# The leading expert's rows gathered after 15 of 20 chunks, the others' tokens placed from SBUF by one-hot matmuls

## Chip, cores and metric

The kernel runs on one core of a Trainium2 chip. The metric is the device time of one execution, in microseconds; the median of three runs is given. A profiled execution of its own gives the trace, and that execution's time stands beside the span of its trace.

## What is computed

Retention attention, then a mixture of experts with one expert per token and a limit of tokens for each, then a gated MLP. Shapes: 4 batches, 8 heads, 576 positions, 64 wide; 2304 tokens of 512; 8 experts with 1024 hidden columns; an MLP with 2048.

```python
def _attn_ref(q, k, v):
    scores = np.matmul(q, k.transpose(0, 1, 3, 2)) / np.sqrt(D_)
    Dmat = np.where(rel >= 0, gamma[:, None, None] ** rel[None], 0.0)
    return np.matmul(scores * Dmat[None], v)

def _moe_ref(x, w_gate, w1, w2, capacity):        # capacity = 2304 // 8 * 2
    logits = x @ w_gate
    expert_idx = np.argmax(logits, axis=1)
    ...                                           # gate_w: softmax at expert_idx
    for i in range(N):
        e = expert_idx[i]
        if counts[e] < capacity:
            disp[e, counts[e]] = x[i]
            pos[i] = counts[e]; counts[e] += 1; keep[i] = True
    h = np.maximum(np.einsum('ecd,edf->ecf', disp, w1), 0.0)
    y = np.einsum('ecf,efd->ecd', h, w2)
    out[i] = gate_w[i] * y[expert_idx[i], pos[i]] # for each kept token

def _moe2_ref(x, w_in, w_out):
    h = x @ w_in
    return (h / (1.0 + np.exp(-1.702 * h))) @ w_out
```

## The kernel before

**Attention.** The tokens go through in 20 chunks `n` (four batches of 128, 128, 128, 128 and 64). SP loads each chunk's q and k (`qk`) and its k and v (`kv`) into buffers that go round, six of each (`load`, L262); POOL scales them (`emit_Q`, L324 and L325). On PE, iteration `n` runs SC of chunk n+1 (scores), XO and KV of chunk n (output and state; the part that comes from the state, L368, is St), and XR of chunk n-1, which transposes the chunk into rows and multiplies it by the gate matrix `iw` in one go (L378). From XR's result DVE takes maxima (`mn`, `lg`), ACT the exponentials (`emit_EX`), and ACT scales the row by its gate weight and writes it to DRAM, tensor `xd` (`emit_ST`). XR of the last chunk takes the PSUM banks that held scores.

**Routing.** Chunks are routed in groups of 5, 5, 5, 3 and 2 (`GROUPS`). `gate1` makes the one-hots of the experts (`OH`). `gate2` counts the tokens ahead of each one by matmuls with a triangle and with ones (`pr`), adds the counts of the groups before (`base`), and makes two factors `A` and `Bt` of one-hots. In `gate3` a few matmuls `ix` multiply these, which puts each token's number at its expert's slot, and DVE adds it to `acc`. With the last group come the index tiles: `IDX0` for the leading expert, `IDX1` for the others, sorted by size (`sort_experts`). The leading expert is fixed by the counts of the first three groups (`lead`, LEAD = 2), so that SP can load its weights; the others come in order of their counts. `pad` strews these steps between the others of the loop; it takes no time of PE but that of the few matmuls.

**Experts.** An expert has a fixed width (`WR`: 370 columns for the first, 344 for the second, ...). POOL gathers its rows out of `xd` with three indirect DMAs (`gather`, L654). PE transposes them into columns (L780 for the first expert, L662 for the others), ACT and DVE split these into a rounded part `xh` and a remainder `xl` (`xevac`). There are 8 steps `fc` for each expert. A step `s` runs `L1` of step s+1 (12 matmuls, L682) and then `L2` of step s (12 matmuls, L701), with weights split in the same way: `split1`, `split2`: ACT casts, `a`, and DVE subtracts, `b`. L1's result is split by ACT (`hi`) and DVE (`lo`). `L2` adds its products up in four banks over the 8 steps (`acc`), and `yevac` takes them out. `load_w(e + 1, fc)` has ACT issue the loads of the next expert's weights, one of eight blocks in each step. Ahead of the first step ACT and DVE load the experts' offsets into registers (`offr`, L786), seven each.

**`compact`.** During the first expert, tokens are also given their places in the sorted order (`PERM`), step by step by `fill(place, 1)` ahead of each L1 and `fill(place, 2)` behind each L2: some 15 operations on DVE, then for each chunk a one-hot of 128 columns (L755, on DVE) and a matmul with it (L758), in a spare corner of `acc`'s first bank:

```python
            for g in range(0, NT + 2, 2):
                for n, (tag, bufs) in zip(range(g, min(g + 2, NT)), (("cu", 3), ("cab", 2))):
                    ...
                    nc.vector.tensor_scalar(As[n], iota, r3[:, n:n + 1], None, op0=ALU.is_equal)
                for n in range(max(g - 2, 0), g):
                    C = CH[n % NC]
                    nc.tensor.matmul(pp, As[n][:C], b2[:C, n, :], start=False, stop=n == NT - 1, skip_group_check=True)
                yield
```

Then the MLP runs over three blocks of 768 tokens, and its rows go out by indirect DMA. Every engine works its instructions off in the order of the program; nothing orders them anew at run time.

Of the kernel before, what the change touches and what calls it, by code (L numbers as in the profile page):

```python
# [1 line left out]

# [29 lines left out]
ZROW = N  # L32
# [5 lines left out]
NW = 3  # L38
# [15 lines left out]
def _consts():  # L54

    if _CONST:
# [10 lines left out]
    valid = np.array([[p < CH[c] for c in range(NC)] for p in range(P)])  # L67
# [9 lines left out]
             ("ca", ca), ("cb", cb), ("ids", ids), ("idz", ids - ZROW), ("idp", np.stack([ids // 16, ids % 16], 2)),  # L77
             ("izp", np.stack([(ids - ZROW) // 16, (ids - ZROW) % 16], 2)), ("iota", iota), ("thr", P * (iota[:, :NR] + 1)),
# [14 lines left out]
def fused(ctx: ExitStack, tc, qk, kv, wg, w1, w2, cap, w_in, w_out, cf, out):  # L93
# [32 lines left out]
    o_s, n_s = at["ca"][0], sum(at[x][1] for x in ("ca", "cb", "ids", "idz", "idp", "izp", "iota", "thr", "e7", "lt8", "tw"))  # L126
# [9 lines left out]
    idz, iota, thr, e7 = table("idz"), table("iota"), table("thr"), table("e7")  # L136
# [93 lines left out]

    with ExitStack() as a:
# [19 lines left out]
        one = acst.tile([P, P], BF16, name="one")  # L251
        St = [acst.tile([P, NP, P], F32, name=f"St{i}") for i in range(3)]
# [7 lines left out]
        def load(n):  # L260
# [23 lines left out]
        nc.gpsimd.memset(acc, float(ZROW))  # L284
# [16 lines left out]
        at_t, xT_t, mn_t, kv_t, xr_t = {}, {}, {}, {}, {}  # L301
# [25 lines left out]
        def emit_SC(n):  # L327
# [4 lines left out]
            sc = ps.tile([P, 2, NP, P], F32, tag="sc", name="sc")  # L332
# [9 lines left out]
        def emit_KV(n):  # L342
# [3 lines left out]
            if c == 0:  # L346
                kv_t[0] = ps.tile([P, NP, D], F32, tag="kv", name="kv")
# [725 lines left out]
```

## Time and profile before

| | |
|---|---|
| median of three runs | 770.02 us (769.84 to 770.62) |
| the profiled execution | 769.79 us, its span 768.0 us |
| TensorE clock granted, mean | 0.983 of full |
| PE busy | 735.1 us, 96% of the span |
| DVE, ACT, POOL busy | 504.4, 353.6, 104.9 us |

The trace holds one execution. Times in it count from the span's start. A stretch's granted clock is a mean share of full speed; 0.50 is the lower of TensorE's two levels, 1.2 of 2.4 GHz. A busy time holds an instruction's latency too, so that two in a row overlap, and the spacing of their starts is shorter.

### The profile page before, as it was taken

The numbers are of one execution on the slowest core, as the hardware profiler recorded it, in microseconds if no ns is written. First come the engines' busy times: TensorE is split into PE (matmuls) and PEld (weight loads), VectorE is DVE, ScalarE is ACT, GpSimd is POOL, SyncE is SP. The second block draws the span as 40 slices with busy tenths as digits, with TensorE's granted clock in tenths as the row PEclk, the third lists the DMA queues.
The fourth block names the chain that finished last, engine by engine and source line by source line (L and its number), as shares of the span: only waits on it lengthen the run. The fifth ranks groups of instructions, "written<-read, shape, count | busy, mean of one in ns | idle before, by whom it ended". The sixth has DMA issues, their size and how long they took to land.

```text
span 768.0 us, 13390 instructions
## 1 busy us (share of the span) xinstructions
PE 735.1 (96%) x4912; PEld 675.2 (88%) x4912; DVE 504.4 (66%) x1233; ACT 353.6 (46%) x754; POOL 104.9 (14%) x120
## 2 busy tenths in 40 slices
PE   6999939999999999999999999999999999999995
PEld 5898828999999999999999999999999988888884
DVE  4455667688988989998988888444434444433442
ACT  4554424365565665665444444433333344333332
POOL 3985025011010010000000000030000012000003
PEclk9999958999999999999999999999999999999998
DMA  9986554366777877867122120020000001000002
GB/s 325 333 294 239 197 166 140 96 216 204 246 220 201 263 241 226 264 219 240 60 68 67 57 70 29 0 83 1 1 0 1 1 18 65 1 1 1 1 0 86
DMA packets 42966, 94.90 MB, mean 124 GB/s; under 512 B 5783, under 2 KB 11031, under 8 KB 42896
## 3 DMA queue, kind: packets, MB, share of 16 engines
q1 hardware_dynamic: 22432, 45.39, 18.1%
q10 hardware_dynamic: 16752, 38.72, 15.8%
q0 software_dynamic: 3712, 9.88, 3.6%
q8 instruction: 41, 0.67, 0.4%
q14 instruction: 29, 0.24, 0.1%
HBM read 79.81 MB, written 14.16 MB: 122 GB/s over the span
## 4 chain that ended last, share of the span: by engine, by line
PE 44%; issue 33%; DVE 5%; POOL 3%; DMA 1%; ACT 1%; ACTq 0%; another core or an unknown queue 0%; DVEq 0%; POOLq 0%
PE h L682 12%; PE acc L701 12%; PE h L854 9%; PE y L879 8%; POOL out L892 2%; PE tx L662 1%; DVE b L633 1%; DMA xg<-xd,IDX 1%; DVE lo L687 1%; DVE b L642 1%; DMA cs<-in_moe_w_in 0%; POOL xg L654 0%; ACT a L632 0%; DVE cab L219 0%; DVE ct L730 0%
## 5 line engine op out<-in xcount | busy, mean ns | idle before, releaser
L860 DVE TENSOR_TENSOR sg<-h,sg 128x384 f32<-128x384 f32 (+1 forms) x96 | 53.4, 557 | 130.7 <-ACT sg L859 130.7
L859 ACT ACTIVATE sg<-h 128x384 f32<-128x384 f32 (+1 forms) x96 | 47.2, 491 | 164.6 <-PE h L854 164.5
L879 PE MATMUL y<-b,gh 128*128 128x512 f32 x288 | 112.5, 391 | 0.0
L879 PE MATMUL y<-a,gl 128*128 128x512 f32 x288 | 112.4, 390 | 0.0
L879 PE MATMUL y<-a,gh 128*128 128x512 f32 x288 | 112.2, 390 | 0.0
L854 PE MATMUL h<-yh,a 128*128 128x384 f32 (+2 forms) x384 | 82.7, 337 | 0.0
L854 PE MATMUL h<-yh,b 128*128 128x384 f32 (+2 forms) x384 | 82.7, 337 | 0.0
L854 PE MATMUL h<-yl,a 128*128 128x384 f32 (+2 forms) x384 | 82.6, 337 | 0.0
L862 ACT CAST gh<-sg 128x384 fp32r<-128x384 f32 (+1 forms) x96 | 49.3, 513 | 71.6 <-DVE sg L860 71.6
L633 DVE TENSOR_TENSOR b<-w1r,a 128x512 fp32r<-128x512 f32 x112 | 77.0, 687 | 7.6 <-ACT a L632 6.4
L701 PE MATMUL acc<-hi,a 128*128 128x370 f32 (+7 forms) x256 | 80.2, 313 | 0.0
L863 DVE TENSOR_TENSOR gl<-sg,gh 128x384 fp32r<-128x384 f32 (+1 forms) x96 | 53.6, 558 | 39.0 <-ACT gh L862 31.2
L701 PE MATMUL acc<-lo,a 128*128 128x370 f32 (+7 forms) x256 | 79.0, 308 | 0.1
L701 PE MATMUL acc<-hi,b 128*128 128x370 f32 (+7 forms) x256 | 78.8, 308 | 0.0
L641 ACT CAST a<-w2r 128x512 fp32r<-128x512 f32 x112 | 69.0, 616 | 20.4 <-PE acc L701 19.3
L642 DVE TENSOR_TENSOR b<-w2r,a 128x512 fp32r<-128x512 f32 x112 | 76.7, 685 | 1.0 <-ACT a L641 1.0
L892 POOL DMA_INDIRECT out<-ob,PERM x18 | 17.8, 990 | 435.2 <-ACT ob L889 431.9
L854 PEld LDWEIGHTS h<-yh,a 128*128 128x128 f32 x384 | 68.2, 188 | 9.1 <-ACT yh L706 0.2
L632 ACT CAST a<-w1r 128x512 fp32r<-128x512 f32 x112 | 69.3, 619 | 12.5 <-issue 3.0
L854 PEld LDWEIGHTS h<-yh,b 128*128 128x128 f32 x384 | 66.4, 188 | 2.7
L854 PEld LDWEIGHTS h<-yl,a 128*128 128x128 f32 x384 | 66.1, 188 | 2.8
L879 PEld LDWEIGHTS y<-a,gl 128*128 128x128 f32 x288 | 54.1, 188 | 11.4
(160 smaller groups left out, 1263.7 us busy)
## 6 DMA issues: line engine op xcount, KB each, us to landing
w1r<-in_moe_w ACTq DMA_DIRECT2D x28, 512.0 KB, 4.4
w2r<-in_moe_w ACTq DMA_DIRECT2D x28, 512.0 KB, 4.0
qk<-in_qk SPq DMA_DIRECT2D x16, 512.0 KB, 6.4
kv<-in_kv SPq DMA_DIRECT2D x16, 512.0 KB, 6.9
cs<-in_moe_w_in SPq DMA_DIRECT2D x32, 256.0 KB, 3.2
cs<-in_moe_w_out SPq DMA_DIRECT2D x32, 256.0 KB, 3.0
xd<-xrow ACTq DMA_DIRECT2D x16, 256.0 KB, 5.4
w1r<-in_moe_w SPq DMA_DIRECT2D x4, 512.0 KB, 5.6
```

What stands on the lines that cost most here:

```text
L632: nc.scalar.copy(a, s)
L633: nc.vector.tensor_tensor(b, s, a, op=ALU.subtract)
L641: nc.scalar.copy(a, s)
L642: nc.vector.tensor_tensor(b, s, a, op=ALU.subtract)
L682: nc.tensor.matmul(h[:, :n], wt[:, kc, :], xs[e, kc][j][:, :n], start=i == 0, stop=i == 3 * KC - 1)
L701: nc.tensor.matmul(y[dc][:, :n], wt[:, dc * P:(dc + 1) * P], x[:, :n], start=fc == 0 and i == 0, stop=fc == NF - 1 and i == 2)
L854: nc.tensor.matmul(h[:, :n], wt[:, kc, :], x[:, kc, o:o + n], start=i == 0, stop=i == 3 * KC - 1)
L859: nc.scalar.activation(sg[:, :n], h[:, :n], AF.Sigmoid, scale=1.702)
L860: nc.vector.tensor_tensor(sg[:, :n], h[:, :n], sg[:, :n], op=ALU.mult)
L862: nc.scalar.copy(gh[:, :n], sg[:, :n])
L863: nc.vector.tensor_tensor(gl[:, :n], sg[:, :n], gh[:, :n], op=ALU.subtract)
L879: nc.tensor.matmul(accs[bi][c // P + t], x[:, t * P:(t + 1) * P], wt, start=f == 0 and i == 0, stop=f == 2 * NF - 1 and i == 2)
```

## The change

The groups are now 5, 5, 5 and 5 chunks. For the first three nothing changes but that their `gate3` comes an iteration earlier. `gate3` of the third group, in iteration 17 behind XR(16), now makes IDX0 and has POOL gather the leading expert's rows from these 15 chunks' part of `xd`. The zero row, which empty slots read, moves to the front of `xd`, so that it lies in that part.

The last five chunks' rows of the leading expert don't pass through DRAM. Their scaled rows `xrow` stay in SBUF (five buffers instead of three), DVE makes the one-hots `A0` of the slots (from 216 on, 154 slots), and PE adds `xrow` transposed times `A0` into the same banks into which it transposes the gathered rows. The remaining routing of the last group (`late_route`: 29 DVE operations, five `ix` matmuls, IDX1 and the sort) runs within the first expert, ahead of `compact`.

```diff
-GROUPS = [(0, 5), (5, 5), (10, 5), (15, 3), (18, 2)]
+GROUPS = [(0, 5), (5, 5), (10, 5), (15, 5)]
+NLEAD = sum(CH[n % NC] for n in range(sum(GROUPS[LEAD])))
+SLEAD = NLEAD // E
...
-            t = rows.tile([P, 2 * DM], F32, tag="qk", name="qk", bufs=6)[:, :2 * NP * C]
+            t = rows.tile([P, 2 * DM], F32, tag="qk", name="qk", bufs=5)[:, :2 * NP * C]
...
-            t = rows.tile([P, 2, H, D], F32, tag="kv", name="kv", bufs=6)
+            t = rows.tile([P, 2, H, D], F32, tag="kv", name="kv", bufs=4)
...
             v.tensor_tensor(acc, acc, ix[:, 1], op=ALU.add)
...
+            if g == LEAD:
+                n = [P, NW, E]
+                ts = sm.tile(n, F32, tag="ts", name="ts", bufs=1)
+                slot = sm.tile([P, NW], F32, tag="slot", name="slot", bufs=1)
+                v.tensor_tensor(ts, top[:, None, :].to_broadcast(n), acc.rearrange("p (e t) -> p t e", t=NW), op=ALU.mult)
+                v.tensor_reduce(slot, ts, op=ALU.add, axis=AX.X)
+                v.tensor_copy(IDX[0], slot)
+                gather(0, xd[:1 + NLEAD, :])
+        def rows_of_lead(x, kc):
+            for t in range(NW):
+                m = min(P, W - t * P)
+                if (t + 1) * P <= SLEAD:
+                    nc.tensor.transpose(x[:, t * P:t * P + m], xg[0, t][:m, kc * P:kc * P + P], ident[:m, :m])
+                else:
+                    nc.tensor.matmul(x[:, t * P:t * P + m], xg[0, t][:m, kc * P:kc * P + P], ident[:m, :m], start=False, stop=False, skip_group_check=True)
...
         emit_EX(NT - 2)
-        emit_ST(NT - 2)
         emit_XR(NT - 1)
-        g = len(GROUPS) - 1
+        emit_EX(NT - 1)
         gate1(g)
-        emit_EX(NT - 1)
-        emit_ST(NT - 1)
...
-        work.append(gate2(g))
-        pad(99)
-        gate3(g)
+        oht = sm.tile([P, KM, E], F32, tag="t", name="oht")[:, :k]
+        v.tensor_tensor(oht, OH[:, t0:t0 + k], top[:, None, :].to_broadcast([P, k, E]), op=ALU.mult)
+        for n in (NT - 2, NT - 1):
+            emit_EY(n)
+        for n in (NT - 2, NT - 1):
+            emit_ST(n)
+        tx0 = [psa.tile([P, 512], F32, tag=f"acc{i}", name="tx0") for i in range(2)]
+        for kc in range(2):
+            rows_of_lead(tx0[kc], kc)
+        pr = ranks(g)
+        rk = RK[:, t0:t0 + k]
+        v.tensor_tensor(rk, pr[:, :k, :], base[:, None, :].to_broadcast([P, k, E]), op=ALU.add)
+        v.tensor_tensor(oht, oht, rk, op=ALU.mult)
+        sl = sm.tile([P, KM], F32, tag="sl", name="sl")[:, :k]
+        v.tensor_reduce(sl, oht, op=ALU.add, axis=AX.X)
+        v.scalar_tensor_tensor(sl, sl, capf, sl, op0=ALU.is_lt, op1=ALU.mult)
...
+        for i, m in ((0, 2), (2, k - 2)):
+            v.tensor_tensor(A0[:, i:i + m], late_s[:, None, :].to_broadcast([P, m, SL]), sl[:, i:i + m, None].to_broadcast([P, m, SL]), op=ALU.is_equal)
...
+        for kc in range(2, KC):
+            rows_of_lead(tx0[kc], kc)
+        for kc in range(KC):
+            for i in range(k):
+                C = CH[(t0 + i) % NC]
+                nc.tensor.matmul(tx0[kc][:, SLEAD:W], xrow_t[t0 + i][:C, kc * P:kc * P + P], A0[:C, i], start=False, stop=i == k - 1, skip_group_check=True)
...
+            for n0, m in ((0, 8), (8, 8), (16, 4)):
...
+                nc.vector.tensor_tensor(A, iota[:, None, :].to_broadcast([P, m, P]), wide(r3, P)[:, n0:n0 + m], op=ALU.is_equal)
...
-        gather(0)
-        place = compact()
+        place = chain(late_route(), compact())
...
-            load_w(e + 1, fc)
+            for i in (fc,) if e else {3: (0, 1), 4: (2, 3), 5: (4, 5), 6: (6,), 7: (7,)}.get(fc, ()):
+                load_w(e + 1, i)
...
             if s < NF:
-                fill(place, 1)
+                fill(place, 5 if s < 3 else 2)
...
             if s < NF:
-                fill(place, 2)
+                fill(place, 5 if s < 3 else 2)
+            if s == 2:
+                gather(1, xd[:, :])
```

What the diff leaves out: `ranks` is the part of `gate2` with the `pr` matmuls; the exponentials of `emit_EX` and the two operations behind them are now `emit_EX` and `emit_EY`; `slots_late` fills the slot numbers `late_s` once, at n = 4. Attention and experts share PSUM banks now: scores, the XR of chunk 18, and two of the four results of an expert take turns in one tile of two banks (`acc2`), `kv` and `xo` in the banks of the other two results. The very first L1 takes its matmuls kc by kc. The registers `offr` are loaded in step 7. The path for tokens above an expert's width changes only in the number of the zero row.

On PE, at the end of attention, what stood between the last XR (L378) and the first L1 (L682) was the index matmuls (L529) of the fourth group, the ranks (`pr`) and index matmuls of the fifth, and the 12 transposes:

```order
L378 MATMUL xr<-iw,xT 64x136 x4
L529 LDWEIGHTS A
L529 MATMUL ix<-Bt,A 128x48
...
L468 MATMUL pr<-OH,tri 128x16
...
L529 MATMUL ix<-Bt,A 128x48
L780 MATMUL tx_1557<-ident,xg 128x128
...
L780 MATMUL tx_1560<-ident,xg 128x114
L682 MATMUL h<-xh,a_1545 128x370 x4
```

Now the transposed rows of kc 0 and 1 stand behind the last XR (L414), ahead of the ranks; those of kc 2 and 3 (`tx_1487`, two banks) and the placement matmuls (L654) stand behind them, ahead of the first L1 (L704):

```order
L414 MATMUL xr<-iw,xT 64x136 x4
L561 MATMUL tx_1459<-ident,xg 128x128
L563 MATMUL tx_1459<-ident,xg 128x128
L563 MATMUL tx_1459<-ident,xg 128x114
...
L482 MATMUL pr<-OH,tri 128x40
...
L561 MATMUL tx_1487<-ident,xg 128x128
...
L654 MATMUL tx_1459<-A_1483,xrow 128x154 x5
L654 MATMUL tx_1460<-A_1483,xrow 128x154 x5
L654 MATMUL tx_1487<-A_1483,xrow 128x154 x10
L704 MATMUL h<-xh,a_1532 128x370
```

So no index matmul stands between attention and the first expert any longer, and the gathered rows do so ahead of the ranks.

On DVE, in the first expert, the end of step 4 and step 5 were, with the weight remainders (L633, L642), `lo` (L687) and the one-hots of four and of two chunks (L755):

```order
L633 TENSOR_TENSOR b_1750<-w1r,a_1749 128x512
L642 TENSOR_TENSOR b_1754<-w2r,a_1753 128x512
L748 TENSOR_TENSOR ct<-ct,sml 128x720
L687 SCALAR_TENSOR_TENSOR lo<-h,hi 128x370
L755 TENSOR_SCALAR A<-sml,r 128x128 x4
L633 TENSOR_TENSOR b_1799<-w1r,a_1798 128x512
L642 TENSOR_TENSOR b_1803<-w2r,a_1802 128x512
L755 TENSOR_SCALAR A<-sml,r 128x128 x2
L687 SCALAR_TENSOR_TENSOR lo<-h,hi 128x370
L755 TENSOR_SCALAR A<-sml,r 128x128 x4
```

Now, at the same two steps, the last operations of `compact` ahead of the one-hots (L825, L828) come only there, and the one-hots (L844) in batches of eight chunks:

```order
L245 TENSOR_TENSOR b_1799<-w1r,a_1798 128x512
L671 TENSOR_TENSOR b_1803<-w2r,a_1802 128x512
L825 TENSOR_TENSOR ct<-r,sml 128x360
L828 TENSOR_TENSOR ct<-ct,sml 128x720
L709 SCALAR_TENSOR_TENSOR lo<-h,hi 128x370
L844 TENSOR_TENSOR A<-sml,r 128x1024
L245 TENSOR_TENSOR b_1843<-w1r,a_1842 128x512
L671 TENSOR_TENSOR b_1847<-w2r,a_1846 128x512
L844 TENSOR_TENSOR A<-sml,r 128x1024
```

So DVE comes to the first one-hot a step and more later, and then does eight chunks at once.

On POOL, ahead of the second expert's gather (indices `IDX_71`), the memset of `yl` stands now where a part of that gather stood, and the first gather (`IDX_70`) is issued behind the last scaling of kv (L361):

```order
L325 TENSOR_TENSOR kv<-kv,tab 128x512
L324 TENSOR_TENSOR qk<-qk,gqs 128x256
L325 TENSOR_TENSOR kv<-kv,tab 64x512
L386 MEMSET mn 128x1
L654 DMA xg<-xd,IDX_70 128x512 x2
L654 DMA xg<-xd,IDX_70 114x512
L654 DMA xg<-xd,IDX_71 128x512 x2
L654 DMA xg<-xd,IDX_71 88x512
L784 MEMSET yl 128x10592
```

```order
L422 MEMSET mn 128x1
L360 TENSOR_TENSOR qk<-qk,gqs 128x256
L361 TENSOR_TENSOR kv<-kv,tab 64x512
L260 DMA xg<-xd,IDX_70 128x512 x2
L260 DMA xg<-xd,IDX_70 114x512
L870 MEMSET yl 128x10592
L260 DMA xg<-xd,IDX_71 128x512 x2
```

So the memset no longer waits behind gathers of the second expert.

## Rows read from the trace of the kernel before

**Rows 1.** Windows: PE, PEld, DVE, ACT, POOL busy, clock, DMA share, GB/s.
```profile
0.00:98.00 98.00, 88.54 (x1227) 81.18 (x1227) 54.28 (x202) 47.98 (x128) 51.43 (x59) 0.99 0.81 280
98.00:116.60 18.60, 6.09 (x31) 4.21 (x29) 11.08 (x57) 4.42 (x12) 5.12 (x5) 0.59 0.46 145
116.60:120.20 3.60, 3.54 (x11) 3.34 (x12) 1.88 (x4) 1.07 (x3) 3.32 (x2) 0.50 0.23 77
160.00:768.00 608.00, 599.04 (x3414) 550.24 (x3412) 407.35 (x897) 282.51 (x579) 34.92 (x51) 0.99 0.31 97
```

**Rows 2.** Timeline of PE: start, us, instruction, what ended the idle time before.
```profile
88.50 1.09 PE L378 MATMUL xr<-iw,xT 128*128 128x136 f32 x8
...
93.08 0.39 PE L529 MATMUL ix<-Bt,A 128*128 128x48 bf16 x5
...
96.17 3.88 PE L378 MATMUL xr<-iw,xT 128*128 128x136 f32 x16 [0.16 <-ACT xrow L409]
...
116.66 1.75 PE L682 MATMUL h<-xh,a 128*128 128x370 f32 x4
...
120.45 0.83 PE L682 MATMUL h<-xh,a 128*128 128x370 f32 x4
...
124.53 0.85 PE L682 MATMUL h<-xh,a 128*128 128x370 f32 x4
...
158.75 0.79 PE L682 MATMUL h<-xh,a 128*128 128x344 f32 x4
```

**Rows 3.** Timeline of POOL, from the gather of the leading expert's rows on.
```profile
110.52 1.14 POOL L654 DMA_INDIRECT xg<-xd,IDX  x1 [0.30 <-issue]
...
117.86 8.98 POOL L784 MEMSET yl<- 128x10592 f32 x1
```

**Rows 4.** The chain that ended last: start, us, what.
```profile
110.52 5.00 DMA xg<-xd,IDX
```

**Rows 5.** Timeline of DVE: routing in the loop, its end, the first expert.
```profile
79.61 0.19 DVE L388 TENSOR_REDUCE gt<-xr 64x8 f32<-64x32 f32 x1 [1.11 <-PE xr L378]
...
80.82 0.20 DVE L422 TENSOR_TENSOR OH<-sml,gt 128x40 bf16<-128x40 f32 x1
...
89.18 0.40 DVE L519 TENSOR_TENSOR Bt<-gt,tok 128x240 bf16<-128x240 f32 x1
...
100.18 0.15 DVE L400 TENSOR_SCALAR mx<-mx 128x1 f32<-128x1 f32 x1 [0.42 <-ACT ex L399]
...
125.11 1.82 DVE L730 TENSOR_SCALAR ct<-RK,capf 128x160 f32<-128x160 f32 x1
...
127.21 0.68 DVE L633 TENSOR_TENSOR b<-w1r,a 128x512 fp32r<-128x512 f32 x1
127.81 0.69 DVE L642 TENSOR_TENSOR b<-w2r,a 128x512 fp32r<-128x512 f32 x1
```

**Rows 6.** DMA issues from 84 to 102 us: KB each, median us to landing.
```profile
xd<-xrow ACTq DMA_DIRECT2D x4, 256.0 KB, 6.5
```

**Rows 7.** One-hots of DVE by form, 37 to 117 us: busy, mean ns | idle.
```profile
L515 DVE TENSOR_TENSOR A<-sml,gt 128x640 bf16<-128x640 f32 x3 | 2.4, 811 | 0.0
...
L515 DVE TENSOR_TENSOR A<-sml,gt 128x256 bf16<-128x256 f32 x1 | 0.4, 420 | 0.0
```

**Rows 8.** Groups of DVE by form, 116 to 160 us.
```profile
L755 DVE TENSOR_SCALAR A<-sml,r 128x128 bf16<-128x128 f32 x20 | 4.7, 281 | 1.1 <-PE acc L758 1.1
L687 DVE SCALAR_TENSOR_TENSOR lo<-h,hi 128x370 fp32r<-128x370 f32 x8 | 4.3, 541 | 7.9 <-ACT hi L686 7.9
...
L748 DVE TENSOR_TENSOR ct<-ct,sml 128x720 bf16<-128x720 f32 x1 | 0.9, 900 | 0.0
```

**Rows 9.** Loads of kv (L269) in the loop, from issue to landing.
```profile
DMA to landing us min/median/max: 4.1/6.8/9.9
```

**Rows 10.** Timeline at the change from the second expert to the third.
```profile
190.47 1.77 DVE L707 TENSOR_TENSOR yl<-acc,yh 128x344 f32 x4
...
192.42 0.31 PE L701 MATMUL acc<-hi,a 128*128 128x324 f32 x1
```

More of the change, by code (lines that the diff above doesn't have):

```diff
@@ L1 @@
 from contextlib import ExitStack
+from itertools import chain
 import numpy as np
@@ L31 @@
 NR = N // P
-ZROW = N
 GW = P + E
@@ L472, in gate2, with tmp @@
             for i in range(k):
-                nc.tensor.matmul(pr[:, NC, :], one, OH[:, t0 + i, :], start=i == 0, stop=i == k - 1, skip_group_check=True)
+                nc.tensor.matmul(pr[:, KM, :], one, OH[:, t0 + i, :], start=i == 0, stop=i == k - 1, skip_group_check=True)
+            return pr
+        def gate2(g):
+            v = nc.vector
+            t0, k = GROUPS[g]
+            GE = [P, k, E]
+            def tmp(name, *n, dt=F32, bufs=2):
+                return sm.tile([P, KM] + list(n), dt, tag=name, name=name, bufs=bufs)[:, :k]
+            oh = OH[:, t0:t0 + k]
+            pr = ranks(g)
@@ L585, in fused @@
             pad(1)
-            if n - 4 in ends:
+            ahead = n - 2 in ends and ends[n - 2] == LEAD
+            if ahead or n - 3 in ends and ends[n - 3] < LEAD:
                 pad(99)
-                gate3(ends[n - 4])
+                if not ahead:
+                    gate3(ends[n - 3])
             for i in {NT - 4: (0, 1, 2), NT - 3: (3, 4, 5), NT - 2: (6, 7)}.get(n, ()):
@@ L593, in fused @@
                 scales(n + 3)
-            if n - 1 in ends and n == NT - 1:
-                work.append(gate2(ends[n - 1]))
-                pad(99)
             if n:
@@ L679, in L1 @@
             i = 0
-            for wt, j in ((a1, 0), (b1, 0), (a1, 1)):
-                for kc in range(KC):
-                    nc.tensor.matmul(h[:, :n], wt[:, kc, :], xs[e, kc][j][:, :n], start=i == 0, stop=i == 3 * KC - 1)
-                    i += 1
+            order = [(wt, j, kc) for wt, j in ((a1, 0), (b1, 0), (a1, 1)) for kc in range(KC)]
+            if e == fc == 0:
+                order.sort(key=lambda x: x[2])
+            for wt, j, kc in order:
+                nc.tensor.matmul(h[:, :n], wt[:, kc, :], xs[e, kc][j][:, :n], start=i == 0, stop=i == 3 * KC - 1)
+                i += 1
             hi = cp.tile([P, W], F32R, tag="hi", name="hi")
@@ L694, in L2 @@
             if fc == 0:
-                yps[e] = [ps.tile([P, 512], F32, tag=f"acc{i}", name=f"acc{i}") for i in range(KC)]
+                yps[e] = banks()
             y = yps[e]
@@ L769, in compact @@
             yield
-        gather(0)
-        place = compact()
+        place = chain(late_route(), compact())
         split1(0, 0)
+        for kc in range(KC):
+            xevac(0, kc, tx0[kc])
         split2(0, 0)
         split1(0, 1)
-        tx0 = [ps.tile([P, 512], F32, tag=f"acc{kc}", name="tx0") for kc in range(KC)]
-        for t in range(NW):
-            m = min(P, W - t * P)
-            for kc in range(KC):
-                nc.tensor.transpose(tx0[kc][:, t * P:t * P + m], xg[0, t][:m, kc * P:kc * P + P], ident[:m, :m])
-        for kc in range(KC):
-            xevac(0, kc, tx0[kc])
-        gather(1)
         nc.gpsimd.memset(yl.bitcast(F32), 0.0)
-        offr = [nc.values_load(posi[0:1, 0, e:e + 1], engines=(ET.Activation, ET.DVE), min_val=0, max_val=N,
-                               skip_runtime_bounds_check_because="a sum of counts of tokens, of which there are N") for e in range(E)]
         steps = [(e, fc) for e in range(E) for fc in range(NF)]
@@ L803, in fused @@
             if s == NF - 1:
+                for _ in place:
+                    pass
+                offr = [nc.values_load(posi[0:1, 0, e:e + 1], engines=(ET.Activation, ET.DVE), min_val=0, max_val=N,
+                                       skip_runtime_bounds_check_because="a sum of counts of tokens, of which there are N") for e in range(E)]
                 for i in range(2):
```

296 lines of the change are left out of this document (162 added, 134 removed).

## The prediction

> **What bounds the kernel now.** I read first the table of stretches [rows 1]. From 160 us to the end PE is busy 599.04 of 608.00 us at a granted clock of 0.99: nothing that happens off PE is won or lost there, and the matmuls of that part stay as they are. The loop of attention ends at about 98. From 98 to 116.6 PE is busy 6.09 of 18.6 us at clock 0.59, and the next 3.6 us run at 0.50. What can be won lies between the last attention matmul and the first expert's second pass, some 20 us.
>
> PE's timeline shows the ends of it [rows 2]: the last two XR from 96.17, L1(0,0) at 116.66, L1(0,1) at 120.45. L1(0,0) takes 3.79 at half clock; L1(0,1) and L2(0,0), 24 such matmuls, take 4.08 at full (120.45 to 124.53), 2.04 each. The rest of the first expert, from 120.45 to L1(1,1) at 158.75, lasts 38.3. The gap itself is the routing of the last five chunks on DVE, then the three gathers by POOL, the last issued at 110.52 [rows 3] and landed 5.00 later [rows 4], then transposes.
>
> **The change up to L1(0,0).** Let P be the moment at which PE has all 370 columns of the leading expert.
>
> The lead's index tile moves to iteration 17, behind XR(16), which ends at 89.59; its five index matmuls take 0.39 [rows 2]. Bt is ready at 89.58, and five small DVE operations of 0.2 follow [rows 5]: IDX0 stands at about 91.2. Each gather holds POOL for 1.14 and 0.30 more [rows 3], so POOL issues at 91.2, 92.65 and 94.0; the last lands at 98.9 by the row of 5.00. But the weights of expert 0 load in this stretch, in which a row write of 256 KB took 6.5 [rows 6]; that gives 100.4. I allow +1.0 (0 to 3) on the result, since the transposes of kc 0 and 1 stand ahead of the rank matmuls in PE's queue, so that a late gather delays the ranks too.
>
> The 0.39 on PE moves the loop's end by 0.45. XR(18) and XR(19), from 96.17 to 100.05 before [rows 2], no longer wait for ACT's row; I put their end at 97.7. Then, by the same operations for five chunks: maxima and gate1 from 79.61 to 81.02, 1.41, with an exp of 0.42 between [rows 5], as its result shares gate1's bank: OH at 99.55. Ranks 0.5: 100.1. The products with the lead's one-hot and four reciprocal operations keep DVE until 100.5, then four small operations: 101.4. A0 is made in pieces of 308 and 462 columns; between 0.420 at 256 and 0.811 at 640 [rows 7] that is 0.47 and 0.63: 101.9 and 102.4. The rows of kc 2 and 3 (1.0) wait for xrow(18), whose bank they take, and end at 102.1. Then 20 placement matmuls of 154 columns in f32: four of 136 columns are 8 instructions in 1.09 [rows 2], 0.23 each without the last one's latency, so 0.26 each and 5.2 together. **P = 107.3**, if the clock holds and the gather is on time.
>
> The clock will hardly hold: PE has little to do from 97.7 to 102, and after such a gap the rows of before show 0.50 for 3.6 us [rows 1]. Work in 3.6 us at half clock would take 1.8 at full, so it costs 1.7 (0 to 5.2, if it were all of the placement). With 1.0 for the gather **P = 110.0**, and L1(0,0), at full clock, ends at 112.05 instead of 120.45: **-8.4**.
>
> The Trainium skill ("TensorE: Matmul & The Clock Gate", What's actually happening) has the throttled state as the default, which activity releases; the 0.50 behind the gap agrees. By that rule placement pays the half rate that L1(0,0) pays now.
>
> **The first expert.** Here the routing that was moved is paid. Before the first 1024-wide one-hot of `compact` is done, DVE has to do the late routing, 29 operations (25 small ones at about 0.23 with issue, A of 640 columns 0.81, Bt 0.40, two on the 21 slots 0.7): 7.7 [rows 5, 7]; fifteen operations of `compact` (L748, the longest, 0.90; the others 0.19 to 0.54), in all 5.6; the one-hot itself, at 1.02 ns a column beyond 640, 1.20; twelve weight remainders, 0.60 from start to start (127.21, 127.81), and six lo, at most 0.54 and 0.45 to the next start: 9.9 [rows 5, 8]. That is 24.4, begun at P + 1.05 behind the four xl, with 0.5 of waits for ACT: **P + 26.0**.
>
> In the 5.6 the tensor_scalar on RK counts 0.35 instead of 1.82. Its long row, 125.11 to 126.93 [rows 5], ends with POOL's memset of yl, 117.86 to 126.84 [rows 3]; after the change it comes near P + 19, when that memset (P + 0.2 to P + 9.2) is over. The Trainium skill ("SBUF — State Buffer", Who interferes with whom) says that a tensor_scalar in a two-port mode and GpSimd exclude each other, and the second is blocked until the first ends; the row agrees. By this rule, were they still to meet, the wait below would be 1.5 longer.
>
> PE meets the first one-hot's matmuls at the start of step 5: 2.05 + 10 x 2.04 + 0.4 for the index matmuls, P + 22.85. So it waits 3.2. Behind it stand six passes of L1 and L2 (12.1), the 20 small matmuls and expert 1's transposes (3.3): P + 41.5, which is 39.4 behind the end of L1(0,0), against 38.3: **+1.1**. The same walk along the queues of before gives 38.4. The batches themselves save DVE work, about 3.1 in place of 4.7 [rows 8], and the register loads now stand in step 7: without the wait the stage would be 2.1 shorter than before.
>
> After a wait of 3.2 the clock can fall once more (+1.7); or DVE, which by the walk ends the expert 1.7 behind PE, its register loads included, holds up a remainder. I take **+1.3** (0 to 2.5).
>
> **At nothing.** Expert 1's gather goes behind IDX1 (P + 14.9) and lands by P + 22.7, its transposes come at P + 26. Expert 1's weights are issued up to P + 18; with the longest landing of the loop's loads, 9.9 [rows 9], they are there by P + 28, needed at P + 31. Two of the four results now share one tile: DVE releases that pair half way through 190.47 to 192.24, at 191.36, and PE takes it at 192.42 [rows 10], 1.0 to spare.
>
> **Sum**: -8.4 + 1.1 + 1.3 = -6.0 from the profiled execution's 769.79 (span 768.0 and 1.8 around it; 0.2 below the median): **763.8 us**.
>
> **Rivals.** (1) *The gather is on time and the clock holds*: P = 107.3, L1(0,0) ends 11.1 earlier, the stage +1.1: 759.8. For it: 0.99 up to 98 and no wait in the loop; against it: 0.59 behind [rows 1]. Chance 0.2.
>
> (2) *The gain is eaten, nothing changes*: all of placement and L1(0,0) at half clock and the gather late: P = 107.3 + 5.2 + 1.0 = 113.5, L1(0,0) ends at 117.3 (-3.1), and a wait longer by a step's part, +2.8: 769.5. For it: half clock until 120.2 before, and the 6.5 of a row write; against it: the transposes and ranks keep PE at work ahead of the placement. Chance 0.2, values from 766 up; 0.12 of it within 0.2% (1.5 us, about what a measurement of this kernel tells from no change).
>
> (3) *Slower: the loop starves on kv.* kv goes from 6 to 4 buffers, so kv(21), say, could be loaded only after KV(17), a microsecond ahead of XR(16) at 88.50, and POOL must have scaled it and the next qk (2.3) by SC(22), which stands three chunks behind SC(19) at 89.5 [rows 2]. At 4.35 a chunk that leaves 12.2 for the landing. It is 6.8 in the median, 9.9 at most [rows 9]. A landing of t sets a pace of (t + 0.8)/3 a chunk: at 14 us 4.93, 0.57 more over 15 chunks, and 763.8 + 8.5 = 772.3. It decides from 13.5 on. For it: the DMA engines are at 0.81 in this stretch [rows 1]; against it: 9.9. Chance 0.08.
>
> **Chances and range.** The forecast, 761.5 to 766, has 0.52. With the rivals: faster by over 0.2% 0.80, within it 0.12, slower 0.08. From 759.3, just beyond rival 1, to 769.3, just short of rival 2, lie 8 in 10.
>
> **What will show it.** Expert 0's gather issued near 91 and landed before 101; the last XR ended near 97.7; ranks at 100 to 101; placement of 5.2 to 9 us; L1(0,0) at 107 to 113; a PE wait of some 3 us at the first matmuls on the 1024-wide one-hot. The prediction is wrong if POOL's issue waits for a row write, if the ranks wait for transposes of rows that land late, if the loop's end moves beyond 98.5, or if DVE falls behind by more than a step in the first expert.

## The result and the profile after

The changed kernel takes 781.01 us in the median of four runs (780.23 to 781.69), the kernel before 769.93 (769.64 to 770.62): a ratio of 1.0142 (1.0125 to 1.016). The forecast was 763.8, so even the direction was wrong. The profiled execution took 781.51 us, its span 779.6 against 768.0, which is 11.6 more.

The stretches of after, in the columns of [rows 1]:

```profile
0.00:98.00 98.00, 85.43 (x1175) 78.31 (x1176) 51.76 (x189) 45.99 (x124) 52.12 (x60) 0.97 0.77 254
98.00:116.60 18.60, 13.95 (x108) 12.13 (x107) 6.00 (x27) 5.53 (x15) 2.63 (x3) 0.82 0.66 246
116.60:120.20 3.60, 3.60 (x22) 2.96 (x22) 0.54 (x1) 0.66 (x2) 0.16 (x1) 1.00 0.00 0
...
160.00:779.00 619.00, 608.41 (x3433) 554.33 (x3431) 410.65 (x903) 283.56 (x585) 35.91 (x52) 1.00 0.30 97
```

The hole behind attention is fuller: PE is busy 13.95 us of 18.6 (6.09 before), and the 3.6 us that ran at 0.50 now run at 1.00. But 5.5 of the 13.95 are the loop itself, which reaches to 104 now. And two stretches changed that the prediction held fixed. In the loop PE is busy 85.43 us instead of 88.54, and behind 160 us it is busy 9.4 us longer; some 3 of these are only work that moved past 160, since the first expert ends 3.2 later.

PE's timeline of after, beside [rows 2]:

```profile
36.02 2.08 PE L372 MATMUL sc<-qk 64*128 64x128 f32 x16 [4.07 <-DVE gt L424]
...
102.88 1.14 PE L414 MATMUL xr<-iw,xT 128*64 128x136 f32 x8 [0.48 <-ACT xT L406]
...
109.31 0.78 PE L563 MATMUL tx<-ident,xg 114*128 114x114 f32 x2 [1.90 <-DMA xg<-xd,IDX]
...
110.93 0.24 PE L482 MATMUL pr<-OH,tri 128*128 128x40 bf16 x1
...
113.04 6.79 PE L654 MATMUL tx<-A,xrow 128*128 128x154 f32 x40
119.76 0.44 PE L704 MATMUL h<-xh,a 128*128 128x370 f32 x1
...
145.46 0.56 PE L836 MATMUL acc<-ct,A 128*128 128x36 bf16 x8 [1.73 <-DVE A L844]
...
164.98 0.42 PE L723 MATMUL acc<-hi,a 128*128 128x344 f32 x1 [0.99 <-DVE yl L729]
```

The first row, SC of chunk 6 in iteration 5, waits for 4.07 us; in the kernel before PE has no wait there. The loop ends 4 us later than before and 6 later than forecast. The gathered rows come late (109.31) and hold up the ranks behind them (110.93). The last row is a wait at the change from the first expert to the second.

The table follows PE through the kernels that matter (from their timelines; us from the span's start, starts unless it says ends). Differences of its rows are used below.

| PE | before | after | e1 | e5 | e8 | e10 |
|---|---|---|---|---|---|---|
| last XR ends | 100.05 | 104.02 | 98.40 | 98.20 | 97.70 | 97.94 |
| ranks of the last group | 102.90 | 110.93 | 104.02 | 104.70 | 100.72 | 101.90 |
| placement | none | 113.04 | 106.36 | 107.14 | 102.65 | 104.35 |
| L1(0,0) | 116.66 | 119.76 | 113.08 | 114.18 | 109.49 | 112.21 |
| L1(1,0) | 154.81 | 158.00 | 151.31 | 150.88 | 147.67 | 148.94 |
| MLP | 361.38 | 368.35 | 361.66 | 357.23 | 358.34 | 355.38 |
| MLP, third block | 622.07 | 633.09 | 626.02 | 621.21 | 623.10 | 616.05 |
| span | 768.0 | 779.6 | 772.6 | 767.6 | 769.6 | 762.0 |

Before against after: L1(0,0) starts 3.10 later; from there to L1(1,0) 38.24 us instead of 38.15, +0.09; experts 1 to 7 +3.78; the MLP to its third block +4.05; the rest +0.6. These add up to the 11.6.

**The loop.** SP's timeline of after (its own columns: start, us of the issue):

```profile
25.67 0.33 SPq L305 DMA_DIRECT2D kv<-in_kv  x1
26.05 1.29 SPq L585 DMA_DIRECT2D sml<-const_f  x1
27.39 0.46 SPq L586 DMA_DIRECT2D capi<-in_moe_capacity  x1
```

and DVE's, of the loop and of the first expert:

```profile
34.11 0.15 DVE L589 CAST capf<-capi 128x1 f32<-128x1 int32 x1 [5.10 <-DMA capi<-in_moe_capacity]
...
137.87 0.30 DVE L810 TENSOR_SCALAR ct<-RK,capf 128x160 f32<-128x160 f32 x1
```

In iteration 2 SP loads chunk 7 and then the constants `sml` and `capi` (before: at 20.94 and 21.42). With four kv buffers chunk 7 takes the buffer of chunk 3, so its load stands at the head of SP's queue until PE is through with that chunk (XO of chunk 3 ends at 25.59), and the constants stand behind it. DVE comes to `capf` at 29, waits 5.10 us for `capi`, and keeps PE's next SC waiting. In the whole loop SP's kv loads wait 46.3 us on XO, in 15 waits of at most 9.8, instead of 6.0 in 3, at most 2.8; its qk loads, which waited 31.9 us in 10 before, wait 7.8 in 8.

**The gather.** DMA issues of after from 84 to 104 us, with KB each and the median to landing:

```profile
w2r<-in_moe_w SPq DMA_DIRECT2D x4, 512.0 KB, 13.1
...
xg<-xd,IDX POOLq DMA_INDIRECT x3, 7.7
```

The third gather is issued at 100.10 and its transposes start at 109.31, 9.2 later, where [rows 4] has 5.00. Half of expert 0's weights land at the same time.

### The profile page after: what moved, and what is told of

Same layout as the page of the kernel before. It is cut to its first block, busy times and chain, and to the rows that moved or that the text cites. A ratio compares the mean times of both kernels' runs of the same rounds, so it can differ in the third digit from the quotient of the medians.

```text
span 779.6 us, 13453 instructions
## 1 busy us (share of the span) xinstructions
PE 749.4 (96%) x4960; PEld 683.7 (88%) x4960; DVE 501.1 (64%) x1204; ACT 351.6 (45%) x754; POOL 105.0 (13%) x120
## 5 line engine op out<-in xcount | busy, mean ns | idle before, releaser
L954 DVE TENSOR_TENSOR gl<-sg,gh 128x384 fp32r<-128x384 f32 (+1 forms) x96 | 53.6, 558 | 38.8 <-ACT gh L953 30.6
L969 PE MATMUL acc<-a,gl 128*128 128x512 f32 x192 | 76.2, 397 | 0.0
L969 PE MATMUL acc<-b,gh 128*128 128x512 f32 x192 | 75.8, 395 | 0.0
L969 PE MATMUL acc<-a,gh 128*128 128x512 f32 x192 | 74.9, 390 | 0.0
L708 ACT ACTIVATE hi<-h 128x370 fp32r<-128x370 f32 (+7 forms) x64 | 27.7, 433 | 57.6 <-PE h L704 54.9
```

The costliest lines, as they stand in the source:

```text
L708: nc.scalar.activation(hi[:, :n], h[:, :n], AF.Relu)
L954: nc.vector.tensor_tensor(gl[:, :n], sg[:, :n], gh[:, :n], op=ALU.subtract)
L969: nc.tensor.matmul(accs[bi][c // P + t], x[:, t * P:(t + 1) * P], wt, start=f == 0 and i == 0, stop=f == 2 * NF - 1 and i == 2)
```

## The experiments

Each kernel differs from the changed kernel (after) or from the experiment named; times are of one run unless a range stands with them. The kernel before took 770.12 beside e1 to e4, 769.51 beside e5 to e8, and 769.48 (769.33 to 770.31) beside e9 to e12. Runs of one kernel differ by 1.5 us in after and by 3.2 in e10, so what an edit is worth is read from the stages of the traces, not from the times alone.

One stage takes two values. Behind the first batch of one-hots, for which PE waits 1.6 to 1.7 us in each of these kernels, the granted clock is 0.66 over 5 us in after, e1, e3 and e8, and the first expert, L1(0,0) to L1(1,0), takes 38.2 us. In e2, e5, e10 and e11 the clock there is 1.00, and it takes 36.7. The runs don't show what decides; 1.5 us of a difference between two single runs can be this alone.

**e1: the constants ahead of the kv load.**

```diff
+            if n == 2:
+                nc.sync.dma_start(sml, cf[:, o_s:])
+                nc.sync.dma_start(capi, cap.bitcast(I32).to_broadcast([P, 2]))
             load(n + 5)
...
-            if n == 2:
-                nc.sync.dma_start(sml, cf[:, o_s:])
-                nc.sync.dma_start(capi, cap.bitcast(I32).to_broadcast([P, 2]))
```

> The changed kernel with the loads of the small constants (sml, capi) issued by SP ahead of the loads of chunk 7 instead of behind them. Theory 1 (the constants stand in SP's queue behind a kv load that waits for one of the four buffers): DVE's wait of 5.1 us for capi and ACT's of 2.8 us for sml are gone, so is PE's wait of 4.1 us at 32 us and the half clock behind it; XR of the last chunk ends near 98 instead of 104, and the time falls by about 6 us, to 775. Theory 2 (the loop starves on late kv and qk landings themselves): the wait moves by a microsecond at most, and the time stays within 1 us of 781.

774.45 us, 6.6 below after. DVE's timeline of e1 at the same instruction, then PE's at the loop's end:

```profile
30.25 0.15 DVE L589 CAST capf<-capi 128x1 f32<-128x1 int32 x1 [0.90 <-DMA capi<-in_moe_capacity]
```
```profile
97.26 1.14 PE L414 MATMUL xr<-iw,xT 128*64 128x136 f32 x8 [0.99 <-ACT xT L406]
...
102.40 0.78 PE L563 MATMUL tx<-ident,xg 114*128 114x114 f32 x2 [0.99 <-DMA xg<-xd,IDX]
...
104.02 0.24 PE L482 MATMUL pr<-OH,tri 128*128 128x40 bf16 x1
```

The constants are issued at 22.28 and 22.75, the wait falls from 5.10 to 0.90, and the last XR ends at 98.40 (forecast: 97.7). SP's kv loads still wait 40.8 us on XO, now at most 3.8 at a time, and PE doesn't feel it: four kv buffers are enough, what stood behind the load was the loss. This is the largest of the causes, and one of order in a queue.

**e2: the ranks ahead of the transposes of kc 0 and 1.**

```diff
         tx0 = [psa.tile([P, 512], F32, tag=f"acc{i}", name="tx0") for i in range(2)]
+        pr = ranks(g)
         for kc in range(2):
             rows_of_lead(tx0[kc], kc)
-        pr = ranks(g)
```

> The changed kernel with the rank matmuls ahead of the transposed rows of kc 0 and 1 in PE's order. If the late landing of the gather (third tile 9.2 us behind its issue) holds up the ranks and with them A0: ranks at 106 instead of 111, A0 ready by 108.5, all four kc's rows transposed behind the landing, placement from about 111.5 instead of 113.0: 1.5 to 2.5 us faster, 778.5 to 779.5. If A0 is not what placement waits for, since rows of kc 2 and 3 end only then: no change.

780.18 us, 0.8 below after and at its lowest run (780.23). PE's timeline of e2:

```profile
106.70 0.18 PE L482 MATMUL pr<-OH,tri 128*128 128x40 bf16 x1 [1.96 <-DVE OH L463]
...
108.79 0.77 PE L563 MATMUL tx<-ident,xg 114*128 114x114 f32 x2 [1.28 <-DMA xg<-xd,IDX]
...
112.49 8.02 PE L654 MATMUL tx<-A,xrow 128*128 128x154 f32 x40
```

The ranks come 4.2 us earlier, the placement 0.55: it adds into banks that must hold the gathered rows first, so it waits for the third tile whatever stands ahead of the ranks. The order on PE was not what cost time, the landing was. Nothing of the 0.55 is left at L1(0,0), which starts at 120.43, 0.67 later than in after, as the placement runs at a clock of 0.84. The 0.8 comes from the first expert (36.7 us instead of 38.2), so from the clock.

**e3: the pair of banks for the last two results instead of the first two.**

```diff
-        return [t[:, 0, :], t[:, 1, :]] + [psa.tile([P, 512], F32, tag=f"acc{i}", name=f"acc{i}") for i in range(2)]
+        return [psa.tile([P, 512], F32, tag=f"acc{i}", name=f"acc{i}") for i in range(2)] + [t[:, 0, :], t[:, 1, :]]
```

> The changed kernel with the four result banks taken in the order acc0, acc1 and then the pair acc2, instead of the pair first. Theory 1 (the order of the banks makes the MLP's second matmuls slower, 9 of them in 2.09 us instead of 2.04): back to 2.04, 4.5 us faster from 368 us on. Theory 2 (it is where the operands lie in SBUF, 64 bytes further on than before): 2.09 stays. In both the first two results of an expert are no longer held back by the pair, so the waits of PE at the start of experts 1, 4, 5 and 6 (about 2.1, 0.4, 0.6, 0.7 us) shrink or move to the third result.

783.47 us, 2.5 above after. PE's timeline of e3 at the first change of expert:

```profile
164.73 0.42 PE L723 MATMUL acc<-hi,a 128*128 128x344 f32 x1 [0.77 <-DVE yl L729]
```

The wait has moved to the seventh matmul of L2, the first into the pair, and each later change of expert has become about 0.5 longer, since the pair, taken out last, is now the last to come free. The pace of the MLP stays. So the order of the banks is not the remedy, and the wait goes with the pair in either place.

**e4: everything behind `sml` moved by 64 bytes.**

```diff
     sml = cst.tile([P, n_s], F32, name="sml")
+    shift = cst.tile([P, 16], F32, name="shift")
```

> The changed kernel with an unused tile of 64 bytes a partition behind the small constants, which moves every later tile of SBUF by 64 bytes, so that the addresses are again an odd multiple of 64, as in the kernel before. Theory 1 (bank order): nothing changes, 2.09 us for 9 matmuls of the MLP's second product. Theory 2 (addresses in SBUF): 2.04 us, and about 4.5 us faster.

779.59 us. It asks why the MLP's second product is slower: 231.9 ns a matmul over the first two blocks, 226.6 before. Here it is 231.7: a shift of all places together is not it.

**e5: e1, and four single banks for an expert's results** (the pool of the pair is closed once the first two `xl` are made, and its two banks are taken as tiles of their own).

```diff
-    psx = pool("psx", space=PSUM)
+    pxs = ExitStack()
+    psx = pxs.enter_context(tc.tile_pool(name="psx", bufs=1, space=PSUM))
...
-        t = psx.tile([P, 2, 512], F32, tag="acc2", name="acc2")
-        return [t[:, 0, :], t[:, 1, :]] + [psa.tile([P, 512], F32, tag=f"acc{i}", name=f"acc{i}") for i in range(2)]
+        return [(psy if i < 2 else psa).tile([P, 512], F32, tag=f"acc{(i + 2) % 4}", name=f"acc{(i + 2) % 4}") for i in range(4)]
...
+        pxs.close()
+        psy = main.enter_context(tc.tile_pool(name="psy", bufs=1, space=PSUM))
```

> As e1 (constants first), and the pair of result banks is given up once the first expert's columns are out of it: from the first L2 on the four results are four tiles of a bank each, in the same order. Theory (the pair is released to PE only when DVE has finished both of its results): the delays of experts 4, 5 and 6 (0.4, 0.6, 0.7 us in the changed kernel) go and most of the 2.1 us of expert 1, so 2 to 3.5 us less than e1's 774.45. Rival (DVE is late there anyway, pair or not): under 1 us.

769.48 us, 5.0 below e1. Experts 1 to 7 take 206.35 us instead of 210.35 (206.57 before): the pair costs 4.0, of which 2.1 lie in expert 1 (32.22 us instead of 34.27). Of the other 1.0, 0.4 lies in the MLP up to its third block, 0.2 behind it, and 0.4 is a balance: L1(0,0) starts 1.1 later, and the first expert is 1.5 shorter, as the windows of e1 and of e5 (columns of [rows 1]) show:

```profile
140.00:155.00 15.00, 15.00 (x91) 14.44 (x90) 7.51 (x17) 5.21 (x12) 3.17 (x3) 0.89 0.44 145
```
```profile
140.00:155.00 15.00, 15.00 (x106) 14.36 (x104) 8.59 (x19) 6.27 (x14) 3.17 (x3) 1.00 0.50 174
```

PE is busy all of both stretches, at a granted clock of 0.89 and 1.00.

What the pair does is plainest on ACT, which copies an expert's results out ahead of DVE's subtractions. ACT's waits in after from 155 us on:

```profile
ACT yh L728 <- DVE yl L729: 7.7, 8, 2.2
```

Once for each expert the copy out of the pair's second result waits for DVE to be done with its first. In the kernel before and in e5, with a tile for each result, no `yh` waits for DVE; in e3 it is the last copy that waits (2.21 at the first change).

**e6: e1, with the remainders `a1` and `b1` in the experts' own pool, as before.**

```diff
-    sp1 = pool("sp1", bufs=2)
...
-        a = sp1.tile([P, KC, P], F32R, tag="a1", name="a1")
-        b = sp1.tile([P, KC, P], F32R, tag="b1", name="b1")
+        a = cd.tile([P, KC, P], F32R, tag="a1", name="a1", bufs=2)
+        b = cd.tile([P, KC, P], F32R, tag="b1", name="b1", bufs=2)
```

> As e1, with the tiles of the L1 weights (a1, b1) allocated behind yl as in the kernel before, which puts them and yl and the conversion buffers back to their old places in SBUF, all of them 64 bytes further on. Theory (where the tiles lie in SBUF sets the pace of the MLP's second product): 9 matmuls back to 2.04 us from 2.09, 4 us less than e1's 774.45. Rival (something else sets it): 2.09 stays, time within 1 us of e1.

773.92 us, only 0.5 below e1, from two opposite effects. The nine matmuls of the second product of the MLP, from their first to the next L1, in after and in e6:

```profile
430.05 0.39 PE L969 MATMUL acc<-a,gh 128*128 128x512 f32 x1
...
432.13 0.86 PE L945 MATMUL h<-yh,a 128*128 128x384 f32 x4
```
```profile
425.53 0.39 PE L968 MATMUL acc<-a,gh 128*128 128x512 f32 x1
...
427.57 0.86 PE L944 MATMUL h<-yh,a 128*128 128x384 f32 x4
```

2.08 and 2.04 us; over two blocks the mean is 226.6 ns a matmul again, and the stretch from the MLP's start to its third block is 2.9 shorter than in e1. On the other side the first expert starts later. ACT's timeline of e6:

```profile
114.33 0.62 ACT L243 CAST a<-w1r 128x512 fp32r<-128x512 f32 x1 [11.56 <-PE tx L653]
```

The experts' pool takes the memory of attention's tiles, `xrow` among them, so the first cast waits for the placement; L1(1,0) starts 2.85 later than in e1.

**e7: the kernel before with the 64 bytes of e4.**

> The kernel before with an unused tile of 64 bytes a partition behind the small constants, so that all later tiles lie where those of the changed kernel begin. If that shift alone slows the MLP's second product: 2.09 us for 9 matmuls instead of 2.04, 4 us slower than the kernel before, 774. If not: 770.

769.58 us, 226.6 ns a matmul: no change, as e4 has it from the other side.

**e8: e1, with the second half of expert 0's weights issued by ACT, behind the routing of the last chunks.**

```diff
-        q = nc.scalar if r else nc.sync
+        q = nc.sync if r == 0 and i < KC else nc.scalar
...
-            for i in {NT - 4: (0, 1, 2), NT - 3: (3, 4, 5), NT - 2: (6, 7)}.get(n, ()):
+            for i in {NT - 4: (0, 1, 2), NT - 3: (3,)}.get(n, ()):
...
+        for i in range(KC, 2 * KC):
+            load_w(0, i)
         for n in (NT - 2, NT - 1):
```

> As e1, with the four w2 blocks of expert 0 (2 MB) issued by ACT at about 99.5 us, behind the gather, instead of by SP from 87 us on. Theory (the gather's last tile lands 8.4 us behind its issue because these 2 MB are on the DMA engines): it lands within 6 us, by 100, the ranks come 2 to 2.5 us earlier, and so does L1(0,0): 772 to 772.5. Rival (the gather is slow by itself, or the late w2 holds up the first L2): no gain or a loss of up to 2 us.

771.53 us, 2.9 below e1. DMA issues of e8 from 84 to 104 us, then PE's timeline:

```profile
w2r<-in_moe_w ACTq DMA_DIRECT2D x4, 512.0 KB, 4.4
...
xg<-xd,IDX POOLq DMA_INDIRECT x3, 5.5
```
```profile
99.86 0.48 PE L563 MATMUL tx<-ident,xg 114*128 114x114 f32 x2 [0.92 <-DMA xg<-xd,IDX]
...
102.65 6.91 PE L656 MATMUL tx<-A,xrow 128*128 128x154 f32 x40
```

The third tile is there 5.7 us behind its issue (94.16) instead of 8.4 in e1 (93.98, 102.40). L1(0,0) starts at 109.49, 3.6 earlier than in e1, and here the clock is at 1.00 from 98 to 113. PE's waits for rows in that stretch are 0.50 and 0.92; in e10 waits of 0.81 and 0.79 were followed by 0.50, so that rows on time keep the clock up is not shown. The placement lasts 6.84 all the same.

**e9: e6 with 384 bytes between `b1` and `a2`.**

```diff
+        if (e, fc) == (0, 0):
+            cd.tile([P, 96], F32, name="apart")
         a = cd.tile([P, DM], F32R, tag="a2", name="a2", bufs=2)
```

> As e6 (constants first, a1 and b1 behind yl), with 384 unused bytes between b1 and a2, so that a2, b2 and all behind them lie 384 bytes further on against a1, b1 and yl. In e6 all four kinds of weight tiles begin at the same place modulo 2048, in e1 a1 and b1 lie 384 bytes off the others. Theory (that offset sets the pace of the MLP's second product): 9 matmuls in 2.09 us as in e1, some 4 us more than e6's 773.9. Rival (it is the place of yl, or of a1 and b1 themselves): 2.04 as in e6.

777.01 us, 3.1 above e6, of which 2.9 lie between the MLP's start and its third block, and the nine matmuls take 2.08 again (231.6 ns each over two blocks):

```profile
430.54 0.40 PE L970 MATMUL acc<-a,gh 128*128 128x512 f32 x1
...
432.62 0.69 PE L946 MATMUL h<-yh,a 128*128 128x384 f32 x3
```

So the place of tiles in SBUF, relative to each other, sets this pace. By the addresses of the compiled programs `a1`, `b1` and `a2`, `b2`, `gh`, `gl` begin at the same place modulo 2048 bytes wherever the mean is 226.6 (before, e6, e7, e10, e12), and 384 bytes apart wherever it is 231.6 to 231.9 (after, e1 to e5, e8, e9, e11). No other offset was tried.

**e11: e1, e5 and e8 together.** 

> As e10 without the move of a1 and b1: constants first, single result banks, w2 behind the gather. If e5 and e8 add up: 774.45 - 5.0 - 2.9 = 766.5, with 2.09 us for 9 matmuls of the MLP's second product. If the gain of e8 is lost again in waits for DVE in the first expert, as DVE's work there is the same: 768 to 769.5.

766.73 us, 2.7 below the kernel before; 774.45 - 5.0 - 2.9 would be 766.5, so the two parts add up in the time. Stage by stage they don't quite: L1(0,0) starts at 111.23, 1.7 later than in e8, and the first expert takes 36.7 us as in e5, not 38.2 as in e8.

**e10: e11, and `a1`, `b1`, `a2`, `b2` in two pools of their own behind `yl`**, so that they have the old places and no tile of attention ahead of them.

```diff
-    sp1 = pool("sp1", bufs=2)
...
+    sp1 = main.enter_context(tc.tile_pool(name="sp1", bufs=2))
+    sp2 = main.enter_context(tc.tile_pool(name="sp2", bufs=2))
     yl = cd.tile([P, KC, N + WR[1]], F32R, name="yl")
...
-        a = cd.tile([P, DM], F32R, tag="a2", name="a2", bufs=2)
-        b = cd.tile([P, DM], F32R, tag="b2", name="b2", bufs=2)
+        a = sp2.tile([P, DM], F32R, tag="a2", name="a2")
+        b = sp2.tile([P, DM], F32R, tag="b2", name="b2")
```

> Constants first, single result banks (e5), w2 of expert 0 behind the gather (e8), and a1, b1 at e6's place, in pools of their own, so that the first cast waits for the loop's loads alone and not for the placement. If the four add up: e1's 774.45 less 5.0 (e5), less 2.9 (e8), less 4.4 (the MLP's pace) = 762, 8 us faster than the kernel before. If e6's slower start of the first expert stays (2.8 us): 765.

763.32 us (761.55 to 764.71, four runs), a ratio of 0.9911 (0.9891 to 0.9932): it beats both kernels. The MLP's pace is 226.6 ns, and its start to third block lasts 260.67 us (260.69 before, 264.74 after, 263.97 in e11).

**e12: e10, with the 20 matmuls on the one-hots of `compact` a step later.**

```diff
-                if n0:
+                if n0 == 16:
                     add(*done.pop(0))
                 yield
+            add(*done.pop(0))
             yield
```

> As e10, with the 20 small matmuls on the wide one-hots put behind L2 of step 5 and after, a step later than the changed kernel has them. Theory (PE's wait of 1.7 us at the first of them, and the half clock of 4 us behind it, are the price of DVE being late there): 3 us faster than e10. Rival (DVE's lag then shows at the next remainder or at yevac): within 1 us of e10.

763.51 us (761.34 to 766.83, five runs): no gain. PE's waits on those one-hots, of e10 and of e12 (us in all, times, the longest):

```profile
PE acc L838 <- DVE A L846: 1.6, 1, 1.6
```
```profile
PE acc L838 <- DVE A L846: 2.0, 2, 1.3
```

The wait is split in two and is no shorter. The half clock of which the theory speaks was not there to be won: in e10's profiled run the clock is 1.00 behind that wait (132 to 150 us), in e12's too.

## Why the prediction was wrong

**Where the sum failed.** Along PE's path the forecast and after part so. The loop ends at 104.02, not 97.7: +6.3, nearly all of it for buffers put at nothing (98.40 in e1). From there to the ranks it takes 6.9, not 3.4: +3.5, a gather allowed for with 1.0. From the ranks to L1(0,1) +0.6, and from there to L1(1,1) -1.3. Behind that +8.4, all put at nothing: the experts 3.8, the MLP 4.05, the rest 0.6. That is the 17.6 between a span of 762.0 and 779.6.

**What held.** The bound was read rightly: the hole behind attention could be won. With the four causes below removed, e10's span is 762.0, 6.0 below 768.0, which is the sum that was forecast. It is not the sum's proof term by term: L1(0,0) starts at 112.21 instead of 110.0, and from there to L1(1,0) it takes 36.7 us where the forecast's own terms give 38.8 (L1(1,1) at 152.75, less 3.94, less 110.0). That these two misses of 2 us cancel is luck. The wait at the first batch of one-hots, +1.3 for its consequences included, was priced at 4.5 and is 1.6 in e10; against that L1(0,0) takes 2.74, not 2.05, because its last `xh` waits for the last placement matmul.

**"At nothing": the buffers in the loop.** Six kv buffers became four, and the only thing weighed was whether kv's own landing would keep up (rival 3, decided "from 13.5 on"). The rival's direction was right and its chain was wrong: no landing was too slow, but SP issues in order, so the kv load that waited for its buffer until 25.67 held up the constants behind it (26.05 and 27.39; 22.28 and 22.75 in e1). The price was 6.6 (e1); 4.1 of it is PE's wait at 36.02, and some 2 are the half clock behind it: the granted clock is 0.50 from 36 to 40 us (SC takes 2.08 instead of 1.16), and KV of chunk 6 starts 6.1 later than in e1 (44.65, 38.53).

**"1.0 to spare" for the pair of banks.** [rows 10] gives the slack at one change of expert, from the second to the third. And it takes DVE's pace from a kernel with a tile for each result, where ACT's copies run ahead of DVE; with the pair ACT waits for DVE once in each expert (7.7 us in 8). At the change from the first to the second, where ACT and DVE also carry `compact` and the split, DVE takes the pair out a microsecond late (the wait of 0.99 above), a `lo` behind it is late (0.51), and expert 1 is 2.1 longer. Experts 1 to 7 together lose 4.0 (e5). The term was not checked at the change that is tightest.

**"The matmuls of that part stay as they are."** They are the same matmuls in number and shape, but not in pace: +4.05 from the MLP's start to its third block. By the spacing of their starts 3.0 of it lies in the second product (e6 and e9 give 2.9 for the place alone) and 1.1 in the first, of which 0.8 is gone with the pair in e5. The diff moved `a1` and `b1` into a pool of their own, and with it their place in memory. The prediction has no term for this.

**The gather's +1.0.** From issue to the third tile's transposes 8.4 us (e1) instead of 5.00, which with the half-clock transposes behind it puts the ranks at 104.0, not at 101.1. Without the term they were forecast at 100.1; 0.7 of the 3.9 to 104.0 is the loop's end (98.40, not 97.7), so the term is 3.2, not 1.0, and just beyond its own upper end of 3. The issue was on time (91.35, 92.72 and 93.98 in e1, against 91.2, 92.65 and 94.0). What delays it is shown by e8: take 2 MB of weights out of its way, and it lands 2.7 earlier. The row of 6.5 for a row write in [rows 6] was too mild a neighbour: the gathers share the DMA engines with loads of `w2r` that take 13.1 us to land in after and 14.3 in e1.

**Placement.** 6.7 to 6.8 us at full clock (119.76 - 113.04, and e8) against 5.2, and no 1.7 for the clock; the sum came out right, 6.9, by luck, from two errors. The weight loads of e8 (PEld's timeline, the first of four like passes) show the first one:

```profile
102.65 1.11 PEld L656 LDWEIGHTS tx<-A,xrow 128*128 128x128 f32 x8
103.92 0.29 PEld L656 LDWEIGHTS tx<-A,xrow 64*128 64x128 f32 x2 [0.16 <-issue]
104.38 1.09 PEld L656 LDWEIGHTS tx<-A,xrow 128*128 128x128 f32 x8 [0.16 <-issue]
```

Eight loads in 1.11, the last one's 0.19 included, are 0.13 apart, and two belong to each matmul, so 0.26 was right for a run of them. But in each of the four passes the loads stop twice, where the chunk of 64 rows begins and where it ends, and from 102.65 to 104.38 a pass takes 1.73 instead of the 1.3 of five matmuls: 1.6 to 1.7 in four. The half clock fell on the transposes ahead (0.50 from 109 to 111 in after).

**The first expert.** From the start of L1(0,1) to L1(1,1) it takes 39.42 in after (122.51 to 161.93); forecast were 39.4 and 1.3 more. The wait for the first batch is 1.73, not 3.2, and half clock behind it follows as allowed for (four matmuls in 1.44, not 0.84, from 146.99). The tensor_scalar on RK takes 0.30 (the row at 137.87) instead of 1.82: POOL's memset runs from 120.04 to 129.00 and is over. The Trainium skill ("SBUF — State Buffer", Who interferes with whom) has such an operation and GpSimd exclude each other; the trace agrees.

The rivals: the first (759.8) is out, since gather and clock both failed it in after; only e8 had the clock. The second, that the gain is eaten at the hole, holds half: in after L1(0,0) starts later than before, but because the loop ends late; with that mended (e1) it starts at 113.08, near the 113.5 of this rival. What would show the prediction wrong was named rightly in two of its four points, the loop's end beyond 98.5 and ranks that wait for late rows. Two slips in the prediction move nothing by more than 0.1: 94.0 and 5.00 make 99.0, not 98.9, and A0's second piece ends at 102.5, not 102.4. Its chunks 21 and 22 are no chunks of this kernel, which ends with 19.

Open is how the place of `a1` and `b1` reaches the matmuls of the second product, which read `a2`, `b2`, `gh` and `gl` only: no run here parts the reads of one engine from the writes of another. Open is also how much of e10's range of 3 us is the clock in the hole, which is 1.00 in e8 and 0.50 from 100 to 106 in e10, and what lets it fall behind a like wait in one kernel and not in another.

## What to carry to other kernels

Fewer buffers can cost more than their own transfers: when a load can wait for a buffer, list what its queue issues behind it and who needs that, before the landing times are weighed. Take the slack of a shared tile at every change of stage and count the tightest, not the one at hand, and look at who else waits for it. And where a diff moves a tile to another pool, its neighbours in memory move too: a stage that is untouched in the program can still change its pace, so compare the spacing of the same matmuls before and after.

## What was not expected of the hardware

The place of tiles in SBUF sets the pace of matmuls here: with 384 bytes between `b1` and `a2`, matmuls of 512 columns start every 231.6 ns instead of 226.6 (e9, e6), 2.2%, some 3 us of this kernel (2.9 between e6 and e9, 3.3 between e11 and e10). A small load can take as long as a large one: in the kernel before `capi`, 1 KB issued at 21.42, takes 6.4 us to land, and a kv load of 512 KB issued 2 us earlier 6.8. In the placement PE stops at each change between weights of 128 and of 64 rows: a pass of ten loads with one chunk of 64 rows among five took 1.73 us instead of 1.3 (e8), at full clock. And the same wait of 1.7 us in the same place is followed by a clock of 0.66 over 5 us in four kernels and by 1.00 in four others.
